# Two FNet layers and two H3 gates on one core: scratch memory laid out anew, sums and normalizations in place, constants by GpSimd transfers

## The chip, the cores and the metric

The kernel runs on one core of one Trainium2 chip. The metric is the device time of one execution in microseconds (us); of the kernel before there are three runs, and their median is 1277.73 us. Lower is better. A core has engines that run their own queues in order: PE (TensorE) multiplies matrices, with its weight loads (PEld) beside it, DVE (VectorE) and ACT (ScalarE) work on rows, POOL (GpSimd) does small work, and SP (SyncE) issues transfers. ACT and POOL can issue transfers too.

## What is computed

x has 2048 rows of 576 numbers. Two layers follow each other, each of an FNet part A and an H3 part B:

```
a = x @ Wd_re.T ; b = x @ Wd_im.T          # x: layernorm of the rows
A(x) = Cr @ a - Ci @ b                      # Cr, Ci: 2048 x 2048 (cos, sin)

kv = (causal conv of k with 4 taps) * v
y  = causal conv of kv with ssm_k (length 2048, per column) + kv * D
B(x) = x * y                                # x: layernorm of the rows

x = x + A(ln(x)); x = x + B(ln(x))          # and the same once more
```

The y of part B depends on k, v and the filters alone. It is the same in both layers and is computed once.

## The kernel before

All products are done in a 32-bit format that PE multiplies at a rounded precision, so each operand is kept in two parts: h, the rounded number, and l, the rest. `split` (line 71) makes them, with an ACT copy (L72) into h and a DVE subtraction (L73) into l. A product is then three matmuls (line 58): h·h, h·l and l·h.

**The first dense layer** (`layer`, line 251) runs over four blocks of 512 output columns (tb), two matrices (g: cos, sin) and 16 row tiles of x (k): 128 steps, counted by n. A step multiplies the row tile X[k] with a 128 x 512 tile of Cr or Ci, 12 matmuls into four accumulators s and two into rm, which gathers the last 64 columns ("rest rows"). The C tiles are loaded two steps ahead (`load_c`, line 172) into three raw slots and split into three cs slots. At the end of a g, `evac_u` (line 211) splits s into U, and `evac_r` (line 216) takes the rest rows: an ACT copy of half of rm (L222) into a tile from the ring `work`, a DVE sum (L223), a split. Then four `hidden` pieces (line 226) per block multiply U with W into the bank bk, add the residual r (L238) into a tile xa, and store it.

X[j] comes from x by `get_x0` (line 498): x(j) lies in one of two `res` slots (`load_x`, L496), is normalized by `normed` for j below 8 (DVE statistics, a power on POOL at L143, an ACT pass at L150 into `work`) or `normed_x` (ACT sums, power at L486, ACT pass at L488), and is split by `to_x` (L155 on ACT, L157 and L158 on DVE).

**The branch** (line 296) computes y beside the first layer, in portions that a schedule by n hands out (line 537 on). Phase 1 (f1, n up to 40): per j a tile of constants f1c (`load_fr`, line 129: a transfer by SP into a landing slot, then an ACT copy, L132), a tile of ssm_k or of k convolved with four taps and multiplied with v (L347, L349, L350 on DVE), a split, 12 matmuls per half, ACT copies into `so` and a store to DRAM (t). Phase 2 (mid, n from 41 to 96): 64 groups load t (L387), split, multiply, combine and store to vd. In n from 41 to 46 W is loaded too. Phase 3 (i2): 16 tiles load vd (L454) and constants, and store y's tiles as yb (L460).

**The handover.** From n = 113 `get_x1` (line 508) makes the second layer's X[j]: it loads xa and yb, `gated` (line 469) forms the gate (statistics L140 to L142, power L143, L474, L475), the result is stored as xb, normalized (L148, L150), stored as y, and split (L155, L157, L158). xa and yb come from the ring `land` (three slots), the two results from the ring `work` (three slots).

**The second layer** computes block 0 as above (`layer(..., 1)`, line 744) and saves U (`save_u`, line 614, L616) and the rest rows (`store_r`, line 619, L622) to DRAM. From n = 14 of it, memory is laid out anew (line 746) and `build` (line 571) forms sums of y tiles for a Strassen scheme, which computes blocks 1 to 3 with seven products instead of eight (line 682). Its C tiles are loaded two at a time by `raw_c` (512 KB), and some are summed (L641, L647). Its results go through slots `both` (2) and `post` (1) to DRAM. Last, 16 `hidden` pieces with `gated` give the output.

**What sets the order.** The text of the kernel gives a first order. The framework then orders each engine's queue by its own estimate, and adds the waits: an instruction that writes a slot waits for all that still read or fill it. `issue_after` keeps a transfer behind another. Rings hand out their slots in turn, so a slot is bound to its last user:

```
    def work():
        return ring["work"]()
...
        tmp = work()[lo:lo + REM, :NT]
        nc.scalar.activation(tmp, ps[NC][other:other + REM], AF.Copy)
        nc.vector.tensor_tensor(tmp, tmp, ps[NC][lo:lo + REM], OP.add)
...
            XL[j] = ring["res"]()
            nc.sync.dma_start(XL[j], x[:, j, :])
```

Of the kernel before, what the change touches and what calls it, by code (L numbers as in the profile page):

```python
# [15 lines left out]
P = 128  # L16
S = 2048
D = 576
# [20 lines left out]
KR = 6  # L39
SMALL = 24  # L40
STATIC = 14
T_FROM = 14
CSB = 5
FLT = 10 * D + 3 * NT
PHW = 8 * D + 112
# [3 lines left out]
def fnet_h3_kernel(ctx: ExitStack, tc: tile.TileContext, x, c_mat, w_re, w_im, k_pad, v, shift_k,  # L49
# [24 lines left out]

    def flat(words, dt, name):
        return sb.tile([P, words], dt, tag=name, name=name)

# [10 lines left out]
    def carve(t, *sizes):  # L88
        at = 0
        for name, words, n in sizes:  # L90
            if name:
                ring.setdefault(name, Ring()).tiles.extend(
                    t[:, at + i * words:at + (i + 1) * words] for i in range(n))
            at += words * n
        assert at <= t.shape[1], (at, t.shape)
# [8 lines left out]
    U_AT = J * 2 * D  # L104
    C_AT = U_AT + 9 * 2 * NT
    mats = flat(C_AT + 6 * NT, FR, "mats")
    xs = mats[:, :U_AT].rearrange("p (j n) -> p j n", j=J)
    flts = flat(4 * SMALL + 8 + FLT, F32, "flts")
    mhalf = flts[:, 4 * SMALL:4 * SMALL + 1]
    carve(flts, ("stat", SMALL, 4))  # L110
    pool = flts[:, 4 * SMALL + 8:]
    carve(pool, ("craw", NT, 3))
    bulk = pool[:, 3 * NT:]
    carve(bulk, ("land", D, 3), ("res", D, 2), ("work", D, 4), ("so", D, 1))
    carve(mats[:, C_AT:], ("cs", 2 * NT, 3))

    def land():
        return ring["land"]()

    def work():  # L120
        return ring["work"]()

    anchor, stored = [], []
# [5 lines left out]
    def load_fr(dst, src):  # L129
        raw = land()[:, :4 * P]  # L130
        nc.sync.dma_start(raw, src.rearrange("p a q -> p (a q)"))
        nc.scalar.activation(dst, raw.rearrange("p (a q) -> p a q", a=4), AF.Copy)  # L132
# [3 lines left out]
    def norm_stats(src):  # L136
# [6 lines left out]
        nc.gpsimd.tensor_tensor(rs, ve, mhalf, OP.pow)  # L143
        return mv, rs, m[:, 16:17]

    def normed(src):
        mv, rs, nb = norm_stats(src)
        nc.vector.tensor_scalar(nb, mv[:, 0:1], rs, -1.0, op0=OP.mult, op1=OP.mult)  # L148
        y = work()
        nc.scalar.activation(y, src, AF.Identity, bias=nb, scale=rs)  # L150
        return y
# [15 lines left out]
    u_d = [dr.tile([9, P, NT], F32, name=f"ud{tb}") for tb in range(TB)]  # L167

# [3 lines left out]
    def load_c(step):  # L172
        g, tb, k = step
        raw = ring["craw"]()[:, :NT]
# [7 lines left out]

    def load_w(im_sign, late=False):
        W.clear()
        for ch in range(9):
            if not late and ch == 0:
                wg = flat(9 * 2 * D, FR, "w").rearrange("p (k n) -> p k n", k=9)
            w = two(xs[:, ch] if late else wg[:, ch])
            raw = (ring["late"] if late else land)()
            load = load_after if late else nc.sync.dma_start  # L190
            if ch < 8:
                src = (w_re if ch < 4 else w_im)[(ch % 4) * P:(ch % 4 + 1) * P, :]
                load(raw, src)
            else:
                load(raw[:REM], w_re[NC * P:, :])
                load(raw[REM:], w_im[NC * P:, :])
            for lo, hi, sg in ((0, P, 1 if ch < 4 else im_sign),) if ch < 8 else ((0, REM, 1), (REM, P, im_sign)):
                if sg > 0:
                    split(w[lo:hi, 0, :], w[lo:hi, 1, :], raw[lo:hi])
                else:  # L200
                    nc.scalar.activation(w[lo:hi, 0, :], raw[lo:hi], AF.Copy, scale=-1.0)
                    nc.vector.scalar_tensor_tensor(w[lo:hi, 1, :], raw[lo:hi], -1.0,
                                                   w[lo:hi, 0, :].bitcast(F32), op0=OP.mult,
                                                   op1=OP.subtract)
# [4 lines left out]
    UT = mats[:, U_AT:U_AT + 9 * 2 * NT].rearrange("p (k a n) -> p k a n", k=9, a=2)  # L209
# [641 lines left out]
```

## Time and profile before

| | |
|---|---|
| three runs | 1276.79, 1277.73, 1282.6 us |
| the profiled execution's own time | 1286.63 us |
| its span, first to last instruction | 1284.6 us |
| mean granted clock of PE | 0.98 |
| matmuls | 6320 (3440 of 512 columns, 2880 of 288) |
| instructions of DVE, ACT, POOL | 1597, 1290, 68 |
| bytes moved | 250.32 MB, 195 GB/s on the mean |

A page of the profile has the busy time of each engine, the same by 40 slices of the span (each digit a tenth), and the granted clock. Other views give the busy time by stretches, what each engine waited for, the chain of waits that ended last, and the instructions in order of time. A line such as "PE s L58 <- DVE mats L158: 2.1, 1, 2.1" says that PE's instruction of line 58 waited for DVE's of line 158, 2.1 us in all, once, at most 2.1 us. Durations of matmuls are those of a pipeline: they overlap, so the time from one start to the next is what a matmul costs.

### The profile page before, as it was taken

Reading aid. Unit: us, or ns where it says so; the run is one execution under the profiler, and the core shown is the slowest. Engines: PE = TensorE matmul, PEld = TensorE weight load, DVE = VectorE, ACT = ScalarE, POOL = GpSimd, SP = SyncE. Lnnn points to the kernel's source line nnn. Section 1 sums busy time; section 2 is a strip of 40 time slices with the busy share of each in tenths; the row PEclk is TensorE's granted clock in tenths of the full one; section 3 lists DMA queues with packets and bytes.
Section 4 is the critical chain, followed back from the end, with each engine's and each line's share of the span. In section 5 each row is a group of like instructions: output and inputs, shape, how many; then the busy total and the mean of one; then the engine's idle time right before and its main releaser. Section 6 shows DMA issues by size and latency. Waiting matters only on the chain.

```text
span 1284.6 us, 18381 instructions
## 1 busy us (share of the span) xinstructions
PE 1210.3 (94%) x6320; PEld 1040.3 (81%) x6320; DVE 866.2 (67%) x1597; ACT 654.2 (51%) x1290; POOL 50.7 (4%) x68
## 2 busy tenths in 40 slices
PE   6799999799999999999999879899999999989998
PEld 5677888698889888789878768787878778779997
DVE  6788895737775697853358865565666657775764
ACT  5775675728865688854553332434443344451200
POOL 1100000000000000000002111000000000000111
PEclk9999999999999999999999989899999989999999
DMA  8968888635544555447878754774375467586642
GB/s 300 294 200 257 280 250 268 201 100 157 164 135 133 147 150 161 146 129 223 260 243 249 218 192 158 232 245 128 115 251 166 132 214 233 153 264 214 205 152 74
DMA packets 140367, 250.32 MB, mean 195 GB/s; under 512 B 15217, under 2 KB 39793, under 8 KB 140274
## 3 DMA queue, kind: packets, MB, share of 16 engines
q1 hardware_dynamic: 106290, 206.68, 52.5%
q10 hardware_dynamic: 33984, 42.48, 9.4%
q8 instruction: 49, 0.80, 0.3%
q14 instruction: 44, 0.36, 0.1%
HBM read 187.76 MB, written 61.34 MB: 194 GB/s over the span
## 4 chain that ended last, share of the span: by engine, by line
PE 53%; DMA 18%; DVE 11%; ACT 9%; issue 6%; POOL 1%; ACTq 0%; SPq 0%; POOLq 0%; DVEq 0%
PE s L58 27%; PE bk L58 23%; PE rm L58 4%; DMA flts<-vd 3%; DMA flts<-in_c_mat 3%; DVE mats L73 2%; DMA flts<-yb 2%; DMA flts<-in_x 2%; DMA t<-flts 1%; ACT mats L72 1%; DMA t<-f1f 1%; DMA flts<-xa 1%; DVE flts L408 1%; ACT flts L401 1%; DMA ud<-ph 1%
## 5 line engine op out<-in xcount | busy, mean ns | idle before, releaser
L58 PE MATMUL s<-mats 128*128 128x512 f32 x2292 | 583.2, 396 | 15.8 <-ACT mats L155 7.7
L58 PEld LDWEIGHTS s<-mats 128*128 128x128 f32 x2292 | 426.5, 190 | 103.1 <-ACT mats L155 10.0
L72 ACT ACTIVATE mats<-flts 128x512 fp32r<-128x512 f32 (+1 forms) x270 | 167.5, 626 | 180.3 <-PE rm L58 113.8
L73 DVE TENSOR_TENSOR mats<-flts,mats 128x512 fp32r<-128x512 f32 (+1 forms) x270 | 183.7, 686 | 81.8 <-ACT mats L72 80.0
L58 PE MATMUL bk<-w,mats 128*128 128x288 f32 x864 | 124.0, 299 | 4.8 <-DVE mats L73 3.0
L58 PEld LDWEIGHTS bk<-w,mats 128*128 128x128 f32 x864 | 119.9, 192 | 7.8 <-DVE mats L73 3.7
L58 PE MATMUL rm<-mats 128*128 128x512 f32 x338 | 107.0, 398 | 8.3 <-DVE flts L223 8.3
L58 PE MATMUL bk<-mid 128*128 128x288 f32 x576 | 97.6, 303 | 14.8 <-ACT mid L72 9.0
L58 PEld LDWEIGHTS bk<-mid 128*128 128x128 f32 x576 | 85.4, 189 | 30.8 <-ACT mid L72 12.4
L58 PE MATMUL s<-t,mats 128*128 128x512 f32 x384 | 99.1, 396 | 2.1 <-ACT ph L616 1.3
L72 ACT ACTIVATE mid<-flts 128x288 fp32r<-128x288 f32 (+1 forms) x128 | 71.7, 563 | 40.6 <-DVE flts L408 35.9
L58 PE MATMUL bk<-mats 128*128 128x288 f32 (+1 forms) x580 | 92.0, 304 | 0.0
L143 POOL TENSOR_TENSOR flts<-flts 128x1 f32<-128x1 f32 x56 | 43.2, 773 | 1199.4 <-DVE flts L142 1188.9
L58 PEld LDWEIGHTS s<-t,mats 128*128 128x128 f32 x384 | 73.1, 191 | 18.7 <-ACT ph L616 1.7
L72 ACT ACTIVATE t<-flts 128x512 fp32r<-128x512 f32 x78 | 48.6, 628 | 73.3 <-PE rm L58 19.4
L58 PEld LDWEIGHTS bk<-mats 128*128 128x128 f32 x580 | 82.3, 189 | 2.4
L73 DVE TENSOR_TENSOR mid<-flts,mid 128x576 fp32r<-128x576 f32 (+1 forms) x128 | 77.0, 606 | 9.2 <-ACT mid L72 5.3
L58 PEld LDWEIGHTS rm<-mats 128*128 128x128 f32 x338 | 64.2, 191 | 22.0 <-DVE flts L223 8.7
L73 DVE TENSOR_TENSOR t<-flts,t 128x512 fp32r<-128x512 f32 x78 | 53.3, 688 | 30.4 <-ACT t L72 30.1
L58 PE MATMUL bk<-f1r 128*128 128x288 f32 x384 | 63.8, 304 | 10.3 <-ACT f1r L72 7.0
L58 PEld LDWEIGHTS bk<-f1r 128*128 128x128 f32 x384 | 59.1, 194 | 17.1 <-ACT f1r L72 7.0
L238 DVE TENSOR_TENSOR flts<-flts,bk 128x288 f32<-128x288 f32 x56 | 25.2, 451 | 54.9 <-PE bk L58 54.6
(112 smaller groups left out, 1327.5 us busy)
## 6 DMA issues: line engine op xcount, KB each, us to landing
flts<-in_c_mat SPq DMA_DIRECT2D x84, 512.0 KB, 4.0
flts<-in_c_mat SPq DMA_DIRECT2D x160, 256.0 KB, 3.6
flts<-t SPq DMA_DIRECT2D x64, 288.0 KB, 2.9
t<-f1f ACTq DMA_DIRECT2D x42, 288.0 KB, 4.3
flts<-in_x SPq DMA_DIRECT2D x32, 288.0 KB, 4.0
vd<-flts ACTq DMA_DIRECT2D x64, 144.0 KB, 3.2
flts<-vd SPq DMA_DIRECT2D x32, 288.0 KB, 3.6
flts<-yb SPq DMA_DIRECT2D x32, 288.0 KB, 3.5
```

The costliest lines, as they stand in the source:

```text
L58: nc.tensor.matmul(ps, lhsT, rhs, start=first, stop=last, skip_group_check=more)
L72: nc.scalar.activation(h, src, AF.Copy)
L73: nc.vector.tensor_tensor(l, src, h.bitcast(F32), OP.subtract)
L143: nc.gpsimd.tensor_tensor(rs, ve, mhalf, OP.pow)
L238: nc.vector.tensor_tensor(xa[:, cs], r[:, cs], ps[:, :HD], OP.add)
L401: nc.scalar.activation(kk[lo, 1, :], pk[hi, :HD], AF.Copy)
L408: nc.vector.tensor_tensor(p1, p1, p2, OP.add)
```

## The change

It lays out scratch memory in another way. The large tiles of x, U and C stay. What else the stages need comes from one tile of floats and two regions, `ra` (41 KB per partition) and `rb` (24 KB), that hold one stage's tiles after another's: ra f1's operands, then W, then t7; rb f1's splits, then mid, then the gate's slots, then ph. With it:

- The rest rows have a tile `rt` of their own (evac_r and store_r).
- A load that is to be split lands in the tile of l itself, and is split there (`split_in`); so do t, vd, the late W and u. There are no landing slots for them.
- f1c and i2c go straight into their operand tiles by transfers that POOL issues, each kept behind the last power issued before; the constants of mid are still loaded by SP and copied.
- x is normalized in its own `res` slot; hidden's sum is written over the residual, the gate over yb, and the second layer's normalized rows over xa.
- xa and yb have five slots each in the handover (two of each where yo was, three in rb), the last stage eight each; mid has three df slots (two before, with three landing slots), i2 four vf slots (two before); post has two slots, block 0's saves eight; k's tiles have four slots (six before), xf three (two before).
- W is copied inside DRAM during n = 47 to 55, and the late W comes from that copy.
- The loads for `build` come at n = 15, 19, 23, 27 and its parts at n = 16 to 31 (14 to 29 before).

In the changed kernel `split` is at lines 76 to 78, the rest rows' copy (was L222) is L237 and their sum L238, hidden's sum L252, x's load L512, its subtractions L161 and L162, the transfers of constants L135 and L137, the gate L491 and L492, block 0's saves L641.

```diff
+    def split_in(h, l):
+        split(h, l, l.bitcast(F32))
...
+    def region_a(dt, name):
+        return sb.tile([P, 9 * 2 * D], dt, tag="ra", name=name)
+    def region_b(dt, name):
+        return sb.tile([P, 6 * WIDE], dt, tag="rb", name=name)
...
-    carve(bulk, ("land", D, 3), ("res", D, 2), ("work", D, 4), ("so", D, 1))
+    lay(flts, 8, ("stat", STAT, 4), ("rt", NT, 1))
...
     def load_fr(dst, src):
-        raw = land()[:, :4 * P]
-        nc.sync.dma_start(raw, src.rearrange("p a q -> p (a q)"))
-        nc.scalar.activation(dst, raw.rearrange("p (a q) -> p a q", a=4), AF.Copy)
+        if pows:
+            with tc.issue_after(pows[-1]):
+                nc.gpsimd.dma_start(dst, src)
+        else:
+            nc.gpsimd.dma_start(dst, src)
...
-        nc.gpsimd.tensor_tensor(rs, ve, mhalf, OP.pow)
+        pows.append(nc.gpsimd.tensor_tensor(rs, ve, mhalf, OP.pow).ins)
...
+    def copy_w():
+        for ch in range(9):
+            if ch < 8:
+                load_after(w_d[ch], (w_re if ch < 4 else w_im)[(ch % 4) * P:(ch % 4 + 1) * P, :])
...
-        tmp = work()[lo:lo + REM, :NT]
+        tmp = ring["rt"]()[lo:lo + REM]
...
-            nc.vector.tensor_tensor(xa[:, cs], r[:, cs], ps[:, :HD], OP.add)
+            nc.vector.tensor_tensor(r[:, cs], r[:, cs], ps[:, :HD], OP.add)
             yield
-        done(j, xa)
+        done(j, r)
...
+        f1r = region_b(FR, "f1r")
+        lay(f1r, 0, ("xf", 2 * D, 3), ("fc", 4 * P, 3))
+        lay(flts, SC_AT + 3 * NT + 3 * D, ("so", D, 3))
+        f1f = region_a(F32, "f1f")
+        lay(f1f, 0, ("k", 2 * D, KR), ("wt", 2 * D, 2), ("tmp", D, 1), ("v", D, 2), ("land", D, 3))
...
+        m1 = region_b(FR, "mid")
+        lay(m1, 0, ("df", 2 * D, 3), ("yf", D, 3), ("mc", 4 * P, 1))
+        lay(flts, SC_AT + 3 * NT, ("res", D, 2), ("kk", D, 2), ("pp", D, 1), ("vo", HD, 3))
...
-            d = land()
-            nc.sync.dma_start(d, t_d[hf][4 * qg:4 * qg + 4].rearrange("q j c s d -> (q j c) (s d)"))
             df = parts("df")
-            split(df[0], df[1], d)
+            nc.sync.dma_start(df[1].bitcast(F32),
+                              t_d[hf][4 * qg:4 * qg + 4].rearrange("q j c s d -> (q j c) (s d)"))
+            split_in(*df)
...
+        lay(m1, 0, ("vf", 2 * D, 4), ("fc", 4 * P, 2))
+        lay(flts, SC_AT + 3 * NT + 2 * D, ("yo", D, 3))
...
-        yb = land()
-        (load_after if late else nc.sync.dma_start)(yb, yb_d[j])
-        q = work()
-        nc.vector.scalar_tensor_tensor(q, xa, mv[:, 0:1], yb, op0=OP.subtract, op1=OP.mult)
+        q = ring["yb"]()
+        (load_after if late else nc.sync.dma_start)(q, yb_d[j])
+        nc.vector.scalar_tensor_tensor(q, xa, mv[:, 0:1], q, op0=OP.subtract, op1=OP.mult)
...
-            X[j] = to_x((normed_x if j >= ASTAT else normed)(XL.pop(j)), j)
+            src = XL.pop(j)
+            X[j] = to_x(normed_x(src, src, ring["junk"]()) if j >= ASTAT else normed(src, src), j)
...
-        xa = land()
+        xa = ring["xa"]()
...
-        y = normed(xb)
+        y = normed(xb, xa)
...
+        if m == 0:
+            lay(flts, SC_AT + 3 * NT + 2 * D, ("xa", D, 2), ("yb", D, 2))
+            lay(region_b(F32, "gate"), 0, ("xa", D, 3), ("yb", D, 3))
...
-        t = ring["post"]()[lo:lo + REM, :NT]
+        t = ring["rt"]()[lo:lo + REM]
...
-            raw = ring["late"]()[:, :NT]
-            load_after(raw, u_d[tb][ch])
-            split(t[:, 0, :], t[:, 1, :], raw)
+            load_after(t[:, 1, :].bitcast(F32), u_d[tb][ch])
+            split_in(t[:, 0, :], t[:, 1, :])
...
-            carve(ph, ("both", wide, 2), ("post", wide, 1), ("late", D, 2))
+            lay(ph, at, ("save", NT, 8))
+            lay(ph, at, ("both", WIDE, 2), ("post", WIDE, 2))
```

## Prediction

> **What bounds the kernel now.** I read the page first: who is busy, and when.
>
> ```profile
> PE 1210.3 (94%) x6320; PEld 1040.3 (81%) x6320; DVE 866.2 (67%) x1597; ACT 654.2 (51%) x1290; POOL 50.7 (4%) x68
> PE   6799999799999999999999879899999999989998
> DVE  6788895737775697853358865565666657775764
> PEclk9999999999999999999999989899999989999999
> ```
>
> PE is the bound, and the changed kernel issues the same 6320 matmuls. So only PE's holes count. In the chain of waits twelve 512-column matmuls take 2.72 us and twelve of 288 columns 1.58 us, so 0.227 and 0.132 us each. 3440 and 2880 of them make 1160 us; the 124 us above that are holes and half clock. The busy time by stage finds them:
>
> ```profile
> 0.00:48.00 48.00, 35.02 (x142) 27.60 (x143) 32.33 (x87) 31.14 (x55) 6.63 (x14) 0.96 0.87 295
> 82.00:224.00 142.00, 138.90 (x733) 120.30 (x734) 115.01 (x172) 87.42 (x193) 0.00 (x0) 0.99 0.85 261
> 224.00:256.00 32.00, 24.40 (x122) 19.88 (x121) 24.23 (x45) 24.15 (x49) 0.00 (x0) 0.95 0.69 207
> 660.00:719.00 59.00, 56.21 (x247) 45.43 (x246) 45.89 (x120) 24.00 (x42) 11.11 (x16) 0.97 0.81 248
> 719.00:760.00 41.00, 29.78 (x155) 26.32 (x154) 29.93 (x74) 13.43 (x21) 5.21 (x8) 0.83 0.60 188
> 1030.00:1040.00 10.00, 7.85 (x21) 5.81 (x21) 6.21 (x9) 4.57 (x8) 0.00 (x0) 0.66 0.56 145
> 1152.00:1281.00 129.00, 126.23 (x909) 123.59 (x907) 79.42 (x162) 17.80 (x30) 15.89 (x16) 1.00 0.52 167
> ```
>
> Columns: stretch, length, PE, weight loads, DVE, ACT, POOL, granted clock, DMA share, GB/s. Holes lie in the start, at 224 to 256 (phase 1 to mid), around 719 to 760 (first to second dense layer), and at spots such as 1030. The last 129 us are full. Then I asked the waits what ends them; the engine that waits is named first.
>
> ```profile
> SPq L496 <- ACT flts L150: 16.5, 7, 4.2
> SPq L496 <- ACT flts L488: 9.1, 5, 3.6
> PE rm L58 <- DVE flts L223: 8.3, 1, 8.3
> ACT ph L622 <- DMA ud<-ph: 7.6, 3, 3.2
> ACT flts L222 <- DMA y<-flts: 1.5, 1, 1.5
> ```
>
> In the start SP waits 25.6 us until a normalization frees an x slot. At 742 PE waits 8.3 us for the rest rows. Three times a rest-row copy waits for a store.
>
> **The change, part by part.** Sum against the profiled execution, 1286.6 us (span 1284.6); the median of the three runs is 1277.7, so I carry the difference over. The order of the changed kernel's queues is known from building it. Its durations are those of these rows.
>
> *Start, x normalized in place.* Now x(j+2) is issued as soon as L150 or L488 of x(j) ends (L150 ends at 9.72, issue at 9.74). In place, the slot is free only after the last subtraction (L158, L162 of the changed kernel). From L150's or L488's end to L158's end lie 2.6 us on the mean of the sixteen. Two slots, seven rounds: up to 18 us by the sixteenth x. Second, DVE's queue changes: ahead of the ninth x's last subtraction stand 8 convolution instructions (L347, L349, L350) now, and 30 in the changed kernel. 22 at 0.75 us are 16.5 us. DVE is busy 32.33 us of the first 48, so between 1 us (it fills every idle moment) and 16.5 come on top. I take 12, since DVE must wait early for a convolution's 576 KB operands (6.4 us to land each) behind the third x's load; the ninth x is then ready at 60 instead of 47.6. By the sixteenth 16 more instructions (12 us) are done than now, and the slots rule again. The two delays overlap, so I take **+14** at the end of the first sixteen steps (bounds +1 and +18). The 16 instructions are then missing from the next stage, where DVE is busy 115 of 142 us and PE stands 2.4 us at 109 and loses 1.7 to half clock: **-4** (0 to -5).
>
> *Constants by GpSimd.* 32 of 33 ACT copies go (L132, 0.628 us each, 20 us). ACT is 51% busy and their stages are held by PE: 0. If ACT were the limit there, -20 would be the far end; I take 0 since PE is busy 138.9 of 142 us. 32 transfers move from SP to POOL, which is 4% busy. No row has a POOL transfer; the same loads on SP land in 3.4 to 4.0 us. With three slots in phase 1 and some 11 us per j they are early, the first alone excepted (a rival below). The 48 powers of L143 that come later stand in POOL's queue behind all the transfers, but are wanted after them.
>
> *Own tile for the rest rows.* At 742 to 750 L222 stands in ACT's queue behind four normalizations and then waits for the store of y that held its work slot. In the changed kernel L237 waits for PE alone and stands right behind the four evictions. But the order pays for this elsewhere: ahead of the *first* eviction stand 11 normalizations instead of 7. One get_x1 costs DVE 4 x 0.42 + 2 x 0.2 + 2 x 0.14 + 2 x 0.81 + 0.21 + 0.22 + 0.68 = 5.1 us. DVE has 66 us of work from the first xa to the split of s0, against 51 now. It cannot start early: the xa and yb slots lie on the yo ring, so one xa load waits for yb's last store (issued at 672.2, 3.9 us) and SP's c loads stand behind it. From 686, where I put that batch, 52 us remain: the split comes near 738 to 742, not at 722.9. Then PE has to do what it now does between 719 and 760: 48 wide and 108 narrow matmuls, 25.1 us. So now it loses 16; then some 18 + 3 (evictions) + 2 (half clock) = 23. **+7** (if DVE filled its idle 13 us, -4; if it works as now, +14).
>
> *Rest rows in the Strassen loop.* The three waits of L622 (3.2, 3.0, 1.4 us) go, since rt's last store is half a block old. At 1031 PE stood 2.2 us and the clock was 0.66 in ten us, thus 6.8 us at half and 3.4 lost: 5.5. At 1128 a c_mat sum (L647) is as late, so about 1. **-6** (-2 to -9).
>
> The Trainium skill, "TensorE: Matmul & The Clock Gate", Part 1, says that PE drops to half after an idle window of about 3.4 us; the 0.66 above agrees, and by this rule the gaps of 1.5 us that I expect at 719 leave the clock whole.
>
> *Landing in split tiles.* W, t and u loads no longer share three or two landing slots. Between 222 and 239 L387's loads go out every 5 us with W loads between them, and PE waits 7.6 us for their splits, 2.8 of it for the first, which stays: **-4** (0 to -7). In phase 3 four vf slots replace two: **-2** (0 to -4). Instructions per split are the same.
>
> *Sums and gate in place.* Same instructions. A residual load must now wait for the store of its slot (3.0 us), two pieces of 3.6 us ahead of its use: 0. If SP held a c load that long, +3 in each layer.
>
> *The switch at n = 14 and the saves.* At 814 to 819 PE waits 4.3 us for L616, which stands behind an ACT copy that waits 5.8 us for a y load. That stays, a step later; eight save slots end one wait of 1.1 us: **-1** (-4 to +4). Ten copies of W inside DRAM (2.65 MB) go where DMA is 43% busy: 0, at most one late load, +3.
>
> Sum: 14 - 4 + 7 - 6 - 4 - 2 - 1 = **+4**: 1290.6 profiled, **1282** as a median (+0.3%).
>
> **The rivals.**
> *Slower: the x slots.* One mechanism: the in-place normalization keeps both x slots, in the first sixteen steps, and nothing is paid back. Price: 18 us instead of 14 - 4, and a handover that starts as late; with the other terms 1290 (with +14 there, 1297). It decides when the ninth x is ready after 60 us. For it: SP's 25.6 us of waits are exactly for these slots. Against: DMA is busy 87% there, so part of the wait is for the bus.
> *Faster: DVE fills its holes.* Start +5 (with the 4 paid back or not), handover -4, all else as above: 1262 to 1266. For it: DVE idles 15.7 of 48 and 13.1 of 59 us. Against: those idle times follow loads, which come later.
> *Late constants.* In ACT's queue the first x's normalization stands behind three evictions of PE's first products, and these need the first constant. POOL's power takes 0.55 us at best and 0.77 on the mean beside DVE; a first transfer stretched as much comes 1 to 6 us late, and all else with it: 1283 to 1288.
> The Trainium skill, "SBUF — State Buffer", "SBUF: two separate sides", says that DVE in a two-port mode keeps GpSimd from writing descriptors, so a POOL transfer waits for DVE; no run so far shows one.
> *It does nothing:* the stores and slots moved were covered: 1278.
>
> **From this to numbers.** Forecast (1276 to 1290) 0.46, slower 0.25, faster 0.18, late constants 0.05, nothing 0.06. A measurement here tells about 0.5%, 6.4 us. The forecast spans that edge; I give 0.26 of it to "the same", 0.18 to "slower", 0.02 to "faster". With late constants half and half, nothing to the same: faster 0.20, same 0.35, slower 0.45. The terms' own ranges, added as independent, are about 11 us; the range **1266 to 1299** leaves out 1 in 10 on each side.
>
> **What would show it.** Right: SP's x loads wait for DVE's last subtraction; PE loses more in the first 100 us; no wait of 8 us for rm, but PE steps of some 4.7 us (now 3.2) ahead of that point; no copy of rest rows that waits for a store; clock whole at the Strassen blocks. Wrong: sixteen x ready by 85 us; or the first eviction of the last block less than 12 us later, measured from the last yb store.

## The result, and the profile after

The changed kernel takes 1283.72 us (median of 18 runs) against 1277.32 of the kernel before (18 runs): a ratio of 1.0041, with a 95% interval from 1.0022 to 1.006. That is 6.4 us slower: the interval does not reach 1, though only just. The forecast was 1282. Its profiled execution took 1285.66 us (span 1283.8), and that of the kernel before 1286.63 (span 1284.6), 9.3 us above its own median. So the two traces together show a gain of 0.8 us where the medians show a loss. The stages have to be compared with more than this one pair of traces.

The page of the changed kernel (busy time of PE and the others, then 40 slices in tenths):

```profile
PE 1210.0 (94%) x6320; PEld 1038.0 (81%) x6320; DVE 866.5 (67%) x1596; ACT 634.4 (49%) x1255; POOL 73.8 (6%) x102
PE   6689999999999999999998899999999999989997
DVE  6867888547885588783257865665667667774664
PEclk9789999999999999999999999999999999999999
```

Its busy time in the same stretches as before (columns as in the prediction):

```profile
0.00:48.00 48.00, 30.37 (x108) 23.17 (x108) 34.93 (x83) 20.54 (x34) 7.48 (x13) 0.93 0.80 271
82.00:224.00 142.00, 137.02 (x716) 117.52 (x715) 110.87 (x173) 87.56 (x192) 9.64 (x18) 0.99 0.82 255
224.00:256.00 32.00, 29.18 (x143) 24.17 (x142) 17.04 (x28) 22.98 (x49) 0.00 (x0) 0.95 0.79 246
660.00:719.00 59.00, 54.64 (x261) 45.59 (x259) 46.21 (x116) 28.36 (x50) 12.70 (x16) 0.97 0.88 285
719.00:760.00 41.00, 36.09 (x175) 30.22 (x176) 31.95 (x86) 16.75 (x26) 9.00 (x11) 0.96 0.71 230
1030.00:1040.00 10.00, 8.75 (x38) 6.65 (x37) 6.81 (x11) 4.89 (x9) 0.00 (x0) 1.00 0.73 222
1152.00:1281.00 129.00, 125.28 (x908) 122.98 (x906) 77.17 (x159) 14.73 (x25) 15.81 (x16) 1.00 0.45 155
```

In the first 48 us PE has issued 108 matmuls, where it had issued 142: the start has become worse. From 719 to 760 it is busy 36.1 us instead of 29.8: the handover has improved. The waits of the changed kernel (who waits, for whom, total, times, longest):

```profile
SPq L512 <- DVE mats L162: 27.1, 14, 3.9
PE s L63 <- ACT mats L159: 19.4, 9, 5.5
ACT flts L647 <- PE rm L63: 8.6, 1, 8.6
PE s L63 <- DVE mats L78: 8.2, 6, 2.8
```

x's loads now wait for DVE's last subtraction, and PE for the split of x. The second layer's copy of rest rows (L647) waits for PE alone, and for no store. No wait of PE for rm is left.

Stretches of fixed length hold other work in each kernel, so the stages are best cut where the program is at the same point. I take the start of ACT's copies of the rest rows: R1 ends the first sixteen steps, R2 to R8 the other halves of the first layer's blocks, S1 the first half of the second layer's block. An x is called ready at the end of DVE's last subtraction for it. What PE loses in a stretch is the stretch's length less 0.227 us for each wide (512 columns) and 0.132 us for each narrow (288 columns) matmul that starts in it. The times between the copies in us, from the trace of each kernel (e1 and so on are the experiments below):

| | to R1 | R1-R2 | R2-R6 (mid) | R6-R7 (i2) | R7-S1 (handover, switch) | S1-end | span |
|---|---|---|---|---|---|---|---|
| before | 84.7 | 82.0 | 378.8 | 113.5 | 163.1 | 462.5 | 1284.6 |
| changed | 105.3 | 77.6 | 377.8 | 109.2 | 154.6 | 459.3 | 1283.8 |
| e2 before, x in place | 95.5 | 76.8 | 376.5 | 112.7 | 160.3 | 459.7 | 1281.5 |
| e8 before, four x slots | 85.2 | 80.3 | 382.9 | 112.7 | 160.3 | 457.1 | 1278.5 |
| e1 four x slots | 83.3 | 77.0 | 376.1 | 110.0 | 152.6 | 458.1 | 1257.1 |
| e5 two slots and two tiles | 91.1 | 77.5 | 378.5 | 109.6 | 153.3 | 456.1 | 1266.1 |
| e6 rest rows shared | 106.4 | 77.0 | 378.8 | 110.0 | 152.4 | 458.8 | 1283.4 |
| e7 two handover slots | 104.7 | 77.8 | 379.0 | 110.1 | 157.2 | 457.3 | 1286.1 |
| e9 both | 105.1 | 78.0 | 377.9 | 111.8 | 167.7 | 458.5 | 1299.0 |
| e10 two split slots | 104.8 | 78.3 | 381.2 | 127.0 | 165.1 | 457.2 | 1313.6 |
| e3 convolution later | 110.8 | 78.4 | 377.3 | 115.1 | 153.1 | 461.4 | 1296.1 |
| e4 constants by SP | 104.5 | 75.0 | 380.9 | 107.9 | 154.9 | 459.7 | 1282.9 |
| e11 four slots, convolution later | 80.0 | 79.6 | 377.7 | 110.4 | 152.8 | 457.1 | 1257.6 |
| e12 nearly no convolution | 89.5 | 91.8 | 380.6 | 109.7 | 156.3 | 459.1 | 1287.0 |

Kernels with the same code in a stage agree within 3 us there in most cases, within some 6 at worst (e3's phase 3 takes 115.1, the changed kernel's 109.2). So a difference of less than that in one stage of one trace tells nothing. Each trace is one execution: those of e1, e2 and e12 are the fastest of their kernel, those of before and e3 the slowest, so whole times are compared by the medians. From R6 on, e2 and e8 are the code of before, and they take 732.7 and 730.1 us, where the profiled execution of before took 739.1. That is most of the 9.3 us by which this execution was above its median.

### The profile page after: what moved, and what is told of

It reads as the page before. It is cut to its first block, busy times and chain, and to the rows that moved or that the text cites. A ratio compares the mean times of both kernels' runs of the same rounds, so it can differ in the third digit from the quotient of the medians.

```text
span 1283.8 us, 18285 instructions
## 1 busy us (share of the span) xinstructions
PE 1210.0 (94%) x6320; PEld 1038.0 (81%) x6320; DVE 866.5 (67%) x1596; ACT 634.4 (49%) x1255; POOL 73.8 (6%) x102
## 4 chain that ended last, share of the span: by engine, by line
PE 65%; DMA 11%; DVE 9%; ACT 8%; issue 3%; POOL 2%; SPq 0%; ACTq 0%; POOLq 0%; DVEq 0%
PE s L63 33%; PE bk L63 26%; PE rm L63 5%; DMA ph<-in_c_mat 3%; DMA t<-flts 2%; ACT mats L77 2%; DVE mats L78 1%; POOL flts L148 1%; ACT mid L77 1%; DVE flts L145 1%; DMA flts<-in_c_mat 1%; DMA mid<-t 1%; DMA flts<-in_x 1%; ACT flts L438 1%; ACT flts L419 1%
## 5 line engine op out<-in xcount | busy, mean ns | idle before, releaser
L63 PE MATMUL s<-mats 128*128 128x512 f32 x2292 | 589.3, 400 | 31.9 <-ACT mats L159 19.4
L77 ACT ACTIVATE mats<-flts 128x512 fp32r<-128x512 f32 (+1 forms) x225 | 140.2, 626 | 163.8 <-PE rm L63 105.4
L78 DVE TENSOR_TENSOR mats<-flts,mats 128x512 fp32r<-128x512 f32 (+1 forms) x225 | 153.6, 685 | 58.7 <-ACT mats L77 57.2
L63 PEld LDWEIGHTS bk<-mid 128*128 128x128 f32 x768 | 111.4, 189 | 34.6 <-ACT flts L438 10.4
L63 PE MATMUL bk<-mid 128*128 128x288 f32 x768 | 126.2, 302 | 13.1 <-ACT flts L438 4.4
L78 DVE TENSOR_TENSOR mid<-mid 128x576 fp32r<-128x576 f32 x96 | 72.4, 756 | 57.5 <-ACT mid L77 56.7
L77 ACT ACTIVATE mid<-mid 128x576 fp32r<-128x576 f32 x96 | 65.4, 684 | 73.9 <-DMA mid<-vd 41.7
L380 ACT ACTIVATE flts<-bk 128x288 f32<-128x288 f32 x128 | 48.5, 409 | 24.1 <-DMA t<-flts 14.3
L77 ACT ACTIVATE mats<-ph 128x512 fp32r<-128x512 f32 x45 | 27.9, 628 | 44.5 <-DVE ph L672 19.3
L63 PE MATMUL bk<-mats,t 128*128 128x288 f32 x336 | 49.4, 295 | 0.0
```

What stands on the lines that cost most here:

```text
L63: nc.tensor.matmul(ps, lhsT, rhs, start=first, stop=last, skip_group_check=more)
L77: nc.scalar.activation(h, src, AF.Copy)
L78: nc.vector.tensor_tensor(l, src, h.bitcast(F32), OP.subtract)
L380: nc.scalar.activation(so[:, c, :], ps[:, :HD], AF.Copy)
```

## The experiments

Theory A: the two x slots, freed only after the last subtraction, set the start, and the other parts gain. Theory B: the convolution's place in DVE's queue sets the start. Theory C: neither; for instance the constants by POOL. Ratios are to the kernel before on the same chip, with 95% intervals.

**e1: four x slots in the changed kernel.**

```diff
-    lay(flts, SC_AT, ("craw", NT, 3), ("res", D, 2), ("junk", D, 1))
+    lay(flts, SC_AT, ("craw", NT, 3), ("res", D, 3))
+    lay(flts, SC_AT + 3 * NT + 6 * D, ("res", D, 1))
...
```

> The changed kernel with four slots for x instead of two (the second pair lies where the rest rows' tile and the junk tile were; that tile moves to the end, and junk into a free part of rb). Everything else is as changed, x is still normalized in place. In the changed kernel the ninth x is ready at 64.7 us and the sixteenth at 99.5 (before: 47.6 and 82.0), and PE loses 47.9 us in the first 128 (before: 31.5). The order that the framework makes of it has 13 convolution instructions ahead of the ninth x's last subtraction in DVE's queue (8 before, 30 changed), and 38 ahead of the sixteenth (25 before, 41 changed). Theory A, the slots set the start: x loads no longer wait for subtractions, the ninth x is ready by 50, the sixteenth by 85, PE loses 34 us or less in the first 128, and the kernel takes some 12 us less than the changed one: 1268 to 1275. Theory B, the convolution in DVE's queue sets it: the ninth x comes early (50 to 53), the sixteenth only 3 us sooner than in the changed kernel (78 us of DVE work ahead of it instead of 81), near 95; 1277 to 1282. Theory C, the constants by GpSimd or the rest of the change cost the time: no difference from the changed kernel, 1281 to 1286.

The rest of the edit moves the rest rows' tile and the junk tile to other places.

Measured: 1262.46 us, ratio 0.9863 (0.9847 to 0.988). The ninth x is ready at 44.0 and the sixteenth at 76.0, and R1 comes at 83.3 instead of 105.3. PE loses 24.9 us in the first 128 instead of 47.9. Theory A stands, and its price was too small: this one edit brings some 21 us. The stretch 48 to 82, first in the changed kernel, then in e1:

```profile
48.00:82.00 34.00, 25.85 (x89) 20.00 (x90) 26.38 (x57) 21.18 (x42) 6.11 (x7) 0.80 0.59 180
```

```profile
48.00:82.00 34.00, 27.97 (x122) 22.01 (x121) 28.76 (x64) 25.22 (x54) 9.30 (x9) 0.95 0.78 232
```

PE's busy time hardly differs, but it does 122 matmuls in it instead of 89. The granted clock was 0.80: PE waits three times there for ACT's copies of x, 2.1 to 3.5 us, and each wait brought a stretch of half clock, 34 x 0.2 x 2 = 13.6 us in all. That is 6.8 us of work lost, against 1.7 in e1. And the DMA share was 0.59, so the transfers had room; what was lacking was a slot to load into.

**e2: the kernel before with x in place, two slots.**

```diff
-            X[j] = to_x((normed_x if j >= ASTAT else normed)(XL.pop(j)), j)
+            src = XL.pop(j)
+            X[j] = to_x(normed_x(src) if j >= ASTAT else normed(src, src), j)
...
```

> The kernel before with one part of the change alone: x is normalized in its own slot instead of into a tile of the ring work; two slots, all else as before. DVE's queue hardly changes: 9 convolution instructions ahead of the ninth x (8 before), 29 ahead of the sixteenth (25 before), DVE work ahead of the sixteenth 71 us instead of 67. Theory A, the slots set the start: each x load waits for DVE's last subtraction, the sixteenth x is ready 12 to 18 us later than the 82.0 of before, the kernel takes 1283 to 1292. Theory B, the convolution in DVE's queue sets it: the sixteenth x comes at most 4 us later, 1276 to 1281. Theory C, neither (the bus is full in the start and hides the slots): within 2 us of before.

Measured: 1289.42 us, ratio 1.0074 (1.0055 to 1.0093), by the medians slower than the whole change. The sixteenth x is ready at 92.8 instead of 82.0. One line of the waits of e2, against L150 and L488 before:

```profile
SPq L496 <- DVE mats L158: 27.1, 14, 5.2
```

The slots alone cost 10.8 us at R1 (95.5 to 84.7). The changed kernel's start is another 9.8 us later, with the same two slots.

**e3: the convolution held back in the changed kernel.**

```diff
             for i in range(2):
+              with tc.issue_after(XI[8]):
                 nc.sync.dma_start(wt[i], bass.AP(tensor=shift_k.tensor, offset=shift_k.offset + 2 * i * D,
...
-            nc.sync.dma_start(XL[j], x[:, j, :])
+            XI.append(nc.sync.dma_start(XL[j], x[:, j, :]).ins)
```

> The changed kernel, two slots for x, with the first load of shift_k (the convolution's weights) held in SP's queue until the load of the ninth x has been issued. So the convolutions come later in DVE's queue: 4 instructions ahead of the ninth x (30 changed), 38 ahead of the sixteenth (41 changed); DVE work ahead of them 33 and 79 us instead of 57 and 81. Theory A, the two slots set the start: x still comes at one load per normalization and subtraction, the ninth x by 60 or later, PE's loss in the first 128 us stays at 45 or more, 1281 to 1287. Theory B, the convolution's place in DVE's queue sets it: the ninth x is ready by 48, the sixteenth near 95, PE loses some 38 us in the first 128, but the 35 convolution instructions that are left must follow soon; 1272 to 1280. Theory C, neither: as the changed kernel, 1281 to 1286, with the ninth x still after 60.

Measured: 1292.28 us, ratio 1.0095 (1.0066 to 1.0124). The ninth x is ready at 57.0 (64.7 changed), but the sixteenth at 106.5 (99.5). Theory B alone falls: with 33 instead of 57 us of DVE work ahead of it, the ninth x came 7.7 us sooner, and the convolutions that follow seem to cost more than that. A's time was missed too.

**e12: nearly no convolution in the first sixteen steps, two slots.**

```diff
-F1_16 = 4
+F1_16 = 1
...
+              with tc.issue_after(XI[15]):
```

> The changed kernel, two slots for x in place, but with nearly no convolution in the first sixteen steps: shift_k's first load is held until the sixteenth x's load has been issued, and the schedule asks for one portion of phase 1 in those steps instead of four. Ahead of the sixteenth x's last subtraction stand 48 us of DVE work with 4 convolution instructions (81 us with 41 in the changed kernel). The convolutions must be done later, so the whole time says less here than the sixteenth x: it was ready at 99.5 in the changed kernel, 92.8 in before with x in place, 82.0 before, 76.0 with four slots. Theory A, two slots in place set a round of their own (load, statistics, power, ACT pass, split, some 10 us for two x), whatever else DVE does: ready at 88 or later. Theory B, DVE's queue sets it: ready by 75. Theory A+B, the convolution stands in each round's chain and lengthens it: ready at 78 to 86. Whole time in each case 1275 to 1300.

Measured: the sixteenth x is ready at 86.7, 0.7 us above the bound of A+B and 1.3 below that of A; the whole 1293.54 us, ratio 1.0093 (1.0058 to 1.0128). So two slots have a pace of their own, which alone is slower than four slots with 78 us of DVE work (76.0). The portions of phase 1 that e12 puts off add 12.8 us to it (99.5): 37 convolution instructions, and with them some splits, products and loads, which no run takes apart from the convolution. How the convolution lengthens a round, one of the changed kernel shows: x's loads go out at 51.80 and 53.25, and DVE then does (start, length, line):

```profile
56.54 0.75 DVE L365 TENSOR_TENSOR f1f<-f1f 128x576 f32<-128x576 f32 x1
57.33 0.76 DVE L366 TENSOR_TENSOR f1f<-f1f 128x576 f32<-128x576 f32 x1
58.00 0.15 DVE L499 TENSOR_SCALAR flts<-flts 128x1 f32<-128x1 f32 x1
...
59.52 0.75 DVE L365 TENSOR_TENSOR f1f<-f1f 128x576 f32<-128x576 f32 x1
60.19 0.15 DVE L501 TENSOR_SCALAR flts<-flts 128x1 f32<-128x1 f32 x1
...
62.31 0.76 DVE L365 TENSOR_TENSOR f1f<-f1f 128x576 f32<-128x576 f32 x1
63.10 0.76 DVE L363 TENSOR_TENSOR f1f<-f1f 128x576 f32<-128x576 f32 x1
63.78 0.15 DVE L501 TENSOR_SCALAR flts<-flts 128x1 f32<-128x1 f32 x1
63.84 0.21 DVE L161 TENSOR_TENSOR mats<-flts,mats 128x64 fp32r<-128x64 f32 x1
63.98 0.69 DVE L162 TENSOR_TENSOR mats<-flts,mats 128x512 fp32r<-128x512 f32 x1
```

x's own steps (L499, L501, L161, L162) take 0.15 to 0.69 us, and those shown stand behind convolutions of 0.75. Only at 64.7 is the slot free and the next load issued. With two slots this chain is the pace. With four, the next x are already loaded, and the sixteenth is ready at 76.0 behind nearly the same convolutions (38 instructions instead of 41). What these cost with four slots no run shows whole: e11 below only moves some of them back.

**e5: the same memory, used in the old way.**

```diff
-            X[j] = to_x(normed_x(src, src, ring["junk"]()) if j >= ASTAT else normed(src, src), j)
+            y = ring["y"]()
+            X[j] = to_x(normed_x(src, y, ring["junk"]()) if j >= ASTAT else normed(src, y), j)
...
```

> The changed kernel with the same extra memory as the four slots, used in the old way: two slots for x, and two more tiles into which x is normalized. So a slot is free at the end of the ACT pass and not after DVE's last subtraction, but only two loads can be under way. Known so far: the copy of the first rest rows (end of the first sixteen steps) comes at 84.7 us in the kernel before, 95.5 in before with x in place, 105.3 in the changed kernel and 83.3 with four slots in place. DVE's work ahead of the sixteenth x's last subtraction stays at 81 us (changed kernel 81, four slots 78). Theory A1, the time of release sets the start: x loads wait for ACT again, that copy comes by 90, 1262 to 1270 us. Theory A2, the number of loads ahead sets it: two slots are too few in either way, the copy comes at 95 or later, 1273 to 1281. Theory B, DVE's queue (81 us of work ahead of the sixteenth x, 41 convolution instructions): the copy stays near 103, 1279 to 1285.

Measured: 1270.46 us, ratio 0.9937 (0.9913 to 0.996); R1 at 91.1. Both lie just above A1's bounds (1270 and 90). Two slots freed early bring some 13 us against the changed kernel, four in place 8 us more. Theory B falls again: 81 us of DVE work ahead of the sixteenth x as in the changed kernel, and it is ready at 85.1 instead of 99.5.

**e8: the kernel before with four x slots in place** (two taken from `work`).

```diff
-    carve(bulk, ("land", D, 3), ("res", D, 2), ("work", D, 4), ("so", D, 1))
+    carve(bulk, ("land", D, 3), ("res", D, 4), ("work", D, 2), ("so", D, 1))
...
```

> The kernel before with x in place and four slots for x in the first stage; the two more are taken from the ring work, which keeps two tiles there (the convolution's result and product, the first rest rows). Nothing else of the change. Order: 8 convolution instructions ahead of the ninth x's last subtraction (8 before), 21 ahead of the sixteenth (25 before). Theory A, the x slots set the start in either layout: the first copy of rest rows comes at 80 to 84 us (84.7 before, 95.5 with two slots in place), and the kernel takes 1268 to 1276, some 12 us less than with two slots in place, with the handover as before (so some 10 us slower than the changed kernel with four slots). Theory D, the new layout makes the gain of the four slots (private rings, or constants by POOL): the copy comes at 88 or later, 1278 to 1288.

Measured: 1280.47 us, ratio 1.002 (1.0001 to 1.0039). Neither theory's line fits whole: R1 at 85.2 is a start like before, 10 us better than with two slots in place, but R1 to R6 takes 463.2 us instead of 453.3 (e2). It had done 21 convolution instructions by the sixteenth x (e1: 38); PE loses 9.1 us from 128 to 224 (e1: 5.6, e2: 2.1). The convolution writes its result and its product into the ring work, which has only two tiles left here in phase 1; whether that is what takes the time was not tried. Against e1, whose start is nearly the same, the rest of the change and these two tiles are worth some 20 us together.

**e11: four slots and the convolution held back.** The edits of e1 and e3 together.

> The changed kernel with four slots for x and shift_k's first load held until the ninth x's load has been issued. DVE's work ahead of the ninth and the sixteenth x: 32 and 73 us (41 and 78 with four slots alone), 5 and 33 convolution instructions. With two slots the same hold cost time (1292.3 against 1283.7), with four slots alone the kernel takes 1262.5. Theory A, the slots are what held the start; with four of them PE waits but 3.5 us for ACT's copies of x in the first 100 us, so the hold brings at most 2 us, and may cost some since the convolutions bunch behind: 1260 to 1270. Theory B, part of the start is DVE's queue: the first copy of rest rows comes at 78 to 80 instead of 83.3, and the time falls to 1256 to 1260.

Measured: 1261.93 us, ratio 0.9842 (0.9811 to 0.9873): e1's time. R1 comes 3.3 us earlier (80.0) and R2 only 0.7. So R1 is where theory B had it and the whole time where theory A had it: what the start gains is gone by R2.

**e4: phase 1's constants by SP and an ACT copy.**

```diff
-                load_fr(fc, f1c[j])
+                raw = ring["fl"]()
+                nc.sync.dma_start(raw, f1c[j].rearrange("p a q -> p (a q)"))
+                nc.scalar.activation(fc, quads(raw), AF.Copy)
...
```

> The changed kernel with the sixteen constants of phase 1 loaded as before: by SP into one of two landing slots, then copied by ACT into the operand tile (0.63 us each). The constants of phase 3 are still loaded by POOL. Two slots for x, in place. The order has 25 convolution instructions ahead of the ninth x (30 changed) and 49 ahead of the sixteenth (41 changed). Theory C, the transfers by GpSimd make the start late (the first constant, or the bus): PE loses some 10 us less in the first 128 us than the 47.9 of the changed kernel, 1270 to 1277. Theories A and B, slots or DVE's queue: the start stays as late, PE loses 45 or more there, and the copies cost little since ACT has room: 1281 to 1289.

Measured: 1285.9 us, ratio 1.0051 (1.0036 to 1.0065), and PE loses 44.6 us in the first 128: no difference from the changed kernel. Theory C falls for the constants.

**e6 and e7: the rest rows' own tile, and the five slots of xa and yb, each taken back.**

```diff
-        tmp = ring["rt"]()[lo:lo + REM]
+        tmp = (ring["yb"]()[:, :NT] if (tb, g) == (TB - 1, 1) else ring["rt"]())[lo:lo + REM]
...
-        t = ring["rt"]()[lo:lo + REM]
+        t = ring["post"]()[lo:lo + REM, :NT]
```

> The changed kernel with the own tile for the rest rows taken back in two places: the last rest rows of the first layer go into the next slot of the ring yb (the gate's), those of the second layer into the ring post. All else as changed. From the seventh copy of rest rows to the first one of the second layer the kernel before takes 163.1 us (before with x in place 160.3) and the changed kernel 154.6; from there to the last one 345.3, 342.6 and 339.6. Theory R, the own tile brings the gain of the handover: PE waits some 5 to 8 us for rm again there, that stretch is back to 160 or more, and three copies wait for stores in the Strassen blocks, 3 to 6 us more in all: 1290 to 1297 us. Theory H, the gain is from the five slots each of xa and yb: the handover stays within 2 us, the Strassen blocks lose 2 to 4: 1283 to 1288.

```diff
             lay(flts, SC_AT + 3 * NT + 2 * D, ("xa", D, 2), ("yb", D, 2))
-            lay(region_b(F32, "gate"), 0, ("xa", D, 3), ("yb", D, 3))
```

> The changed kernel with two slots each for xa and yb in the handover instead of five each (the three and three in rb are left out; the others are those where yo lay). The rest rows keep their own tile. Theory H, the number of slots gives the changed kernel's steady steps there: with two each the loads of the next tile start only when a tile's store has landed, one tile takes 7 us or more instead of some 5, the stretch from the seventh copy of rest rows to the first of the second layer grows from 154.6 to 162 or more: 1290 to 1300 us. Theory R, the own tile of the rest rows gives the gain: the stretch grows by 3 us or less, 1281 to 1287. The forecast's own view (DVE's 63 us of work ahead of the eviction is the limit, whatever the slots) gives the same as R.

Measured: e6 1284.06 us, ratio 1.0046 (1.0028 to 1.0064); e7 1286.54 us, ratio 1.0053 (1.0032 to 1.0074). R7 to S1 is 152.4 and 157.2 (154.6 changed). In neither does PE wait for rm, and e6 loses nothing from S1 on (458.8). So either part can be left out, and the 8.3 us stay away.

**e9: both taken back at once.** The edits of e6 and e7 together.

> The changed kernel with both handover parts taken back at once: the last rest rows go into the next slot of the ring yb (and into post in the second layer), and xa and yb have two slots each. Each alone cost nothing that could be told: PE has no wait for rm in either, while it waits 8.3 us there before and 9.1 in before with x in place. Theory E, either one suffices (with five slots the slot that the rest rows get has been stored long ago; with two, the own tile has no other user): with neither, the copy stands behind a store again, PE waits 5 to 9 us for rm, the stretch from the seventh copy of rest rows to the first of the second layer grows from 154.6 (157.2 with two slots) to 162 or more: 1290 to 1297 us. Theory N, the gain there has another source (normalizing over xa and the gate over yb, so that two places serve a tile where four served it): the stretch stays at 158 or less, 1283 to 1289.

Measured: 1305.69 us, ratio 1.0192 (1.0155 to 1.023), R7 to S1 167.7. Theory E, at twice its price. The wait of PE, and ACT's queue in e9 (start, length, line):

```profile
PE rm L63 <- DVE flts L238: 16.6, 1, 16.6
```

```profile
752.11 0.87 ACT L154 ACTIVATE flts<-flts 128x576 f32<-128x576 f32 x1 [12.50 <-DVE flts L153]
...
765.44 0.87 ACT L154 ACTIVATE flts<-flts 128x576 f32<-128x576 f32 x1 [10.02 <-DVE flts L153]
...
768.43 0.59 ACT L237 ACTIVATE flts<-rm 64x512 f32<-64x512 f32 x1
```

ACT's queue has the copy behind normalizations, and two of these wait 12.5 and 10.0 us for tiles that are loaded late: from 690 to 790 SP's loads of xa wait 6.7 us for stores of y and 4.4 us for stores of xa that hold their slots. That the framework put the copy there because its slot in the ring of two comes free late is likely, but was not tested.

**e10: two split slots in phases 2 and 3.**

```diff
-        lay(m1, 0, ("df", 2 * D, 3), ("yf", D, 3), ("mc", 4 * P, 1))
+        lay(m1, 0, ("df", 2 * D, 2), ("yf", D, 3), ("mc", 4 * P, 1))
...
-        lay(m1, 0, ("vf", 2 * D, 4), ("fc", 4 * P, 2))
+        lay(m1, 0, ("vf", 2 * D, 2), ("fc", 4 * P, 2))
```

> The changed kernel with two slots instead of three for the split tiles of phase 2 (df) and two instead of four for those of phase 3 (vf), so as many as before; loads still land in the tile of l, and there are no landing slots. From the sixth to the seventh copy of rest rows (phase 3) the kernel before takes 113.5 us (112.6 and 112.7 in its two variants), the changed kernel and its variants 109.2 to 110.1. PE loses 10.8 and 8.2 us at 224 to 256 before, 5.5 changed. Theory L, the count of slots gives both gains: with two a load can start only when the split of the tile two earlier has been multiplied, phase 3 takes 113 to 118, phase 2 loses another 2 to 6: 1287 to 1297 us. Theory M, the gain comes from not sharing a landing slot with W's and other loads: within 2 us of the changed kernel, 1282 to 1287.

Measured: 1315.72 us, ratio 1.026 (1.0224 to 1.0296). R6 to R7 takes 127.0 us (109.2), R7 to S1 10.5 more; R2 to R6 3.4 more, which is within theory L's 2 to 6 but hardly more than the same code differs by, and PE loses 4.7 us from 224 to 256 (5.5 changed). Theory L for phase 3, well above its price: 17.8 us there instead of 4 to 9. e10's waits from 560 to 692:

```profile
SPq L464 <- PE bk L63: 24.5, 19, 4.4
SPq L464 <- DVE mid L78: 17.0, 9, 4.5
```

```profile
PE bk L63 <- ACT mid L77: 10.7, 9, 3.0
```

The same wait of PE in the changed kernel, from 560 to 670:

```profile
PE bk L63 <- ACT mid L77: 1.4, 2, 1.0
```

A load that lands in l's own tile must wait until PE has used both parts (L464 for PE). With the landing slots of before (the load of vd, L445 there) it waited for the split alone. In the changed kernel L464 waits 28.5 us for PE too, but four slots hide it. Two tiles that are landed in are worth less than the two of before, which had landing slots beside them.

## Why the prediction came out right

The time and the sign came out as forecast, but that is in part luck: the two largest terms were wrong, in opposite directions. The start cost some 7 us more than taken, and the handover gained where a loss was forecast. The terms against the trace of before and, from R6 on, against the mean of e2 and e8, whose code there is the old one:

| term | predicted | against before's trace | from R6: against e2, e8 |
|---|---|---|---|
| start, to R1 | +14 | +20.6 | |
| payback, R1-R2 | -4 | -4.4 | |
| landing in mid, R2-R6 | -4 | -1.0 | |
| landing in i2, R6-R7 | -2 | -4.3 | -3.5 |
| handover and switch, R7-S1 | +7 - 1 | -8.5 | -5.7 |
| rest rows in Strassen, S1-end | -6 | -3.2 | +0.9 |
| sum | +4 | -0.8 | +6.9 |

With the last column in place of the rows from R6 on, the sum is 6.9 us, and the medians differ by 6.4. Single stages are known to some 3 us at best, so that the two lie this close is chance as well.

**Start.** The mechanism was right, both its parts. The size was not: the step that failed is that the two delays overlap and make +14; 20.6 lies above the bound of 18. The slots cost 10.8 (e2) and the rest 9.8; they add up, since convolutions stand inside the round of two slots (e12). The constants are not that rest (e4), but e12 puts off other work of phase 1 too, so how much of the 9.8 is the convolution alone is not shown. The rival of the slots was to be decided by a ninth x that is ready after 60 us: it was ready at 64.7. But 4.4 us were paid back, and the handover's gain went against the rest of it.

**Payback.** The size was right, its reason was not shown. The prediction put it down to convolutions that are done early: 41 of them have started by R1 in the changed kernel, 26 before. But e2 has started only 30 by R1, and takes 76.8 us from R1 to R2, less than the changed kernel's 77.6.

**Handover.** Here the mechanism failed, and not only a size. DVE's work was judged rightly: from the last yb store to the first eviction 63.1 us (679.1 to 742.3) instead of 47.1, and ACT's passes come every 5.0 us on the mean (696.7 to 741.5). But the loss for PE, some 18 us and 3 and 2 more, was wrong. The two stretches of before, then those of the changed kernel, up to the first eviction and behind it:

```profile
672.20:719.30 47.10, 46.47 (x203) 37.83 (x203) 39.96 (x109) 17.84 (x28) 10.56 (x15) 0.98 0.82 251
719.30:760.00 40.70, 29.48 (x153) 26.02 (x152) 29.63 (x72) 13.12 (x21) 5.21 (x8) 0.83 0.60 187
```

```profile
679.10:742.30 63.20, 54.61 (x240) 43.99 (x239) 54.55 (x159) 24.12 (x36) 18.54 (x23) 0.96 0.85 279
742.30:768.00 25.70, 25.70 (x142) 22.82 (x142) 16.70 (x39) 9.74 (x17) 3.10 (x4) 0.96 0.52 173
```

In those 63.1 us PE did 202 wide and 36 narrow matmuls, 50.5 us, so it lost 12.7. Then, from 742.3 to 768.0, it lost 1.3. That is 14.0 us where 23 were forecast; before, it lost 1.9 in the 47.1 us and 16.4 from 719.3 to 760. I took the narrow matmuls for work that is left until after the eviction; 30 more of them than before (36 instead of 6) filled the slower steps. The rest of the gain from R7 to S1 lies ahead of the last yb store, where PE lost 4.1 us before and 1.0 after, and behind the stretches shown, up to S1 (6.2 and 3.7). As for the wait for rm, either the own tile or the five slots keep it away (e6, e7), and without both it is back (e9): the own tile is enough, but not needed, as I had it.

**Strassen.** The copies of rest rows wait for no store, as predicted; it brings nothing that can be told. PE's 2.2 us and the half clock at 1031 were counted as the price of L622's waits. But in e2 these waits are as long as before (7.6 us in all) with the clock whole there, and e6 shares a tile again (of two, where before had one) and loses nothing. So the term of -6 was given for waits that cost next to nothing.

**Landing.** From 224 to 256 PE lost less (10.8 us before and 8.2 in e2, which has the old code there; 5.5 after), but it lost some 3 us more from 256 to 576; why is open. The whole stage R2 to R6 takes 377.8 us, 378.8 before and 376.5 in e2: no gain that can be told, where -4 was taken. In phase 3 the gain was 3.5 to 4.3 us, more than the 2 taken, and it hangs on the four vf slots (e10). **Constants:** at nothing that can be told, as taken (e4; PE waits 1.8 us for them in all). The first is not late, since PE's first matmul starts at 6.57 us (7.00 before).

## What to carry to other kernels

Work in place makes a slot's life longer, so the saved memory must go back into more slots of the same ring: here four slots instead of two turned a loss of 0.4% into a gain of 1.4%. Where a ring with few slots paces a chain, work put into the queue of one of its engines can lengthen every round (12.8 us for sixteen x here); with four slots the sixteenth x was ready 23.5 us sooner behind nearly the same work. An engine's wait that ends in the same us as PE's hole is not its price: take it away in a second kernel, or look for an execution without the hole, before it goes into a sum.

## What the runs showed of the hardware

A constant of 256 KB issued by POOL takes 5.3 us (median) from issue to landing, and 3.5 when SP issues it (e4). Each issue takes 0.53 to 0.69 us of POOL. The Trainium skill, "SBUF — State Buffer", "SBUF: two separate sides", has DVE's two-port modes keep GpSimd from writing descriptors; the longest of these 34 issues on POOL shows at most 0.16 us of that. Whether some of the 1.8 us more to landing is of that kind, no view tells.

Half clock followed shorter gaps of PE than I expected. In the changed kernel, gaps of 2.81 us (up to 700.7) and 2.08 (up to 740.9) brought it: the granted clock was 0.56 and 0.59 in the two us each from 700 to 704, and 0.50 from 742 to 744. A gap of 1.29 (up to 265.4) left it whole. So did one of 2.64 us in the kernel before (up to 227.55) and one of 3.04 in e2 (up to 1128.1), so the length of a gap alone does not decide. The traces show what does. In all fourteen the granted clock changes only at the edges of windows of 3.41 us, which follow each other without a break. Of the windows at whole clock (from 20 us after the start to 12 us before the end), all 81 in which PE stood for more than 0.57 of the window were followed by half clock, and none in which it stood for less than 0.43; in between there were both. The 2.64 us fell into two windows, 0.46 and 0.31 of them. The Trainium skill, "TensorE: Matmul & The Clock Gate", Part 1, has the clock fall after an idle window of about 3.4 us; here a window that is idle for somewhat more than half of its time is enough. The prediction saw this rule confirmed at 1031, but PE stood there for 2.15 us only, 0.56 of a window.
